# Token loads in 1 KB pieces and whole-array spare matmuls in the head of a fused attention + SwiGLU kernel

## The chip, the cores and the metric

The kernel runs on one core of one Trainium2 chip. A core has five engines that run side by side, each with its own in-order instruction stream: TensorE (PE in the profile, with its weight loads as PEld), VectorE (DVE), ScalarE (ACT), GpSimd (POOL) and SyncE (SP), which here only issues DMAs. The metric is the device time of one execution in microseconds (us); lower is better. The time of the kernel before is 1207.22 us, the median of three runs (1205.26 to 1208.33).

## The reference

One input x of 2048 tokens by 512 features (bf16) goes through a layer norm, and its result xn through two blocks whose outputs are added to x:

```python
xn = _layernorm(x, axis=-1)
return x + _A_ref(xn, A_wqkv, A_wo) + _B_ref(xn, B_w1, B_w3, B_w2)
```

Block A is attention with 32 heads of 16 features: `qkv = xn @ wqkv`, softmax of `q k^T / 4` over all 2048 keys for each head, times v, then `@ wo`. Block B is a gated MLP with 1792 hidden features: `(silu(xn @ w1) * (xn @ w3)) @ w2`. No position enters anywhere, so a fixed permutation of the tokens changes nothing but the place of the output rows.

## The kernel before

**Tiling.** The tokens are 16 tiles of 128. Scores are made twice. In the first pass ("p1") a tile of 128 queries stands as weights and the keys stream past; DVE takes the maximum of each row out of PSUM (line 1040, one reduce for 1024 score columns, 1018 reduces in the record). The maxima go as two more rows into the queries, so that in the second pass ("p2", line 1262) the scores come out transposed and shifted, and ACT only has to take the exponential (lines 1275 and, for two PSUM banks at once, 1305). Then TensorE multiplies with V, and FFN and output matmuls fill what time TensorE has left. The work is cut into units, (query chunk of 512, group of 4 heads, query range); the first three units of the kernel are 128, 128 and 256 queries of the first group.

**Who sets the order.** The order of every engine's instructions is computed when the kernel is built, by a list planner inside `_build`. It keeps a clock per engine (`P.free`), a cost for each instruction (`occ`, `lat`, `_c_mm` and its like for matmuls) and a readiness for each datum, and in a loop it takes from the candidates of all engines (`pick_dve`, `pick_act`, `pick_pe`, `pick_pool`, `pick_sp`) the one that can start first. On the chip each engine then runs its list in order, and semaphores keep the data right; an instruction that the planner expected early and that is late holds up all behind it on its engine.

**The head.** SP issues the loads in this order: token tiles 0-1, 2-3, 4-7 (`load_x`, line 472), the weights of K and of Q (line 476), token tiles 8-11, 12-15, the weights of V; then the first two tiles of x for the residual (`load_xr`, line 845), four pieces of FFN weights and four DRAM fills (lines 493 and 496). For each load the planner adds its KB over `DMA_RATE` (GB/s) to a running landing time that begins at `DMA_FIRST`:

```python
def load(fn, keys, kb):
    landed[0] += kb / DMA_RATE
    P.dma(fn, writes=keys, lat=max(2.2, landed[0] - P.free["sp"]), occ=0.54)
```

Layer norm statistics of tiles 0 to 7 are on DVE (`bn_stats`, line 576, `bn_aggr`, line 579), those of tiles 8 to 15 on ACT (two sums, lines 566 and 570); POOL makes the factors (lines 589 and 592), DVE normalises tiles 0 to 7 (line 605) and POOL the others (line 615). TensorE transposes a normalised tile (line 638), ACT copies it to `xnT` (line 645). With tiles 0 to 3 there, TensorE makes K (`KT0`) and Q (`QT0`) of the first group for the first 512 tokens, four column groups of 32 at a time (line 545, `col_groups`), ACT copies them (lines 661 and 757), and the first p1 scores (line 1000) and the first reduce (line 1040) follow.

**Spare matmuls.** While TensorE has nothing to do ahead of `QT0`, the planner gives it matmuls whose results nobody reads (`warm_cand`, called by `fill_cand` and `pick_pe`): on a free bank, the all-ones tile as weights and as data. Each is one planner item of a column group, that is four matmul instructions of 128x32 weights and 128 columns, each with its weight load, which run side by side in the four column strips of the array. The planner counts `_c_mm(128)`, doubled before its time 5.9 (`_COLD`). `note_load` keeps a sliding sum of streamed columns; ahead of `QT0` nothing is decided by it.

**Which token is where.** Tile t holds in partition p the token 512*(t//4) + 4*p + t%4. Two neighbouring tiles of a load are then 2 KB in a row in DRAM for each partition, four are 4 KB. `load_xr` and `store` move one tile each, with 1 KB per partition, 4 KB apart in DRAM.

## Time and profile before

| what | value |
| --- | --- |
| median of three runs | 1207.22 us (1205.26 to 1208.33) |
| the profiled execution | 1208.99 us |
| its span, first to last instruction | 1207.3 us |
| mean granted TensorE clock | 0.996 of full |
| busy: TensorE, DVE, ACT, POOL | 96%, 97%, 97%, 38% of the span |
| DMA packets, bytes | 129842, 52.90 MB |

The profile is one execution on the chip. "Busy" is the time in which an engine has an instruction in work; a busy TensorE need not be at its peak. A row of the costly groups gives line, engine, operation, output and input with their shapes, and a count, then busy time, mean length in ns, and the idle time of that engine just before these instructions with what ended it. "issue" as that releaser means that the engine waited for nothing that the profile shows. The granted clock is what the throttle left of TensorE's full speed.

### The profile page before, as it was taken

To read this page: it belongs to the slowest core of one execution; us is meant where nothing else is said; L and a number is where in the kernel's file an instruction comes from. 1 tells how busy PE (TensorE), PEld (TensorE's weight loads), DVE (VectorE), ACT (ScalarE), POOL (GpSimd) and SP (SyncE) were. 2 spreads that over 40 slices of the span, in tenths; PEclk is the share of its full clock that TensorE was granted. 3 is DMA by queue.
4 is the path that set the end of the run, shared out by engine and by line. 5 is a ranking of instruction groups with operands and counts; after the bars stand their busy time and mean duration, and the time that the engine had idled before them with its cause. 6 is when DMAs were issued, how large, how long until landed. Compare 5 with 4: busy or idle time off the path is not lost.

```text
span 1207.3 us, 45302 instructions
## 1 busy us (share of the span) xinstructions
PE 1153.4 (96%) x19827; PEld 482.5 (40%) x19827; DVE 1174.8 (97%) x1069; ACT 1176.5 (97%) x2307; POOL 455.1 (38%) x908
## 2 busy tenths in 40 slices
PE   7999999999999999999999999999999999999997
PEld 4444343343334443443333333333333333345554
DVE  5999999999999999999999999999999999999994
ACT  5899999999999999999999999999999999999997
POOL 3435554535322245454222146553122126233320
PEclk8999999999999999999999999999999999999999
DMA  5342313222101122121001112211000111000000
GB/s 171 106 73 65 88 37 92 49 54 52 30 20 29 36 50 53 39 54 29 22 16 27 37 43 66 47 41 34 22 21 16 36 38 34 23 22 21 23 12 25
DMA packets 129842, 52.90 MB, mean 44 GB/s; under 512 B 100084, under 2 KB 129004, under 8 KB 129644
## 3 DMA queue, kind: packets, MB, share of 16 engines
q1 hardware_dynamic: 129644, 50.01, 16.5%
q8 instruction: 155, 2.54, 0.9%
q14 instruction: 43, 0.35, 0.1%
HBM read 38.73 MB, written 6.74 MB: 38 GB/s over the span
## 4 chain that ended last, share of the span: by engine, by line
PE 40%; ACT 40%; DVE 15%; issue 3%; POOL 2%; DMA 1%; ACTq 0%; SPq 0%; POOLq 0%
ACT PT L1275 29%; PE ps L545 22%; DVE part L1040 14%; PE ps L1262 11%; PE ps L1000 6%; ACT PT L1305 4%; ACT th L815 1%; ACT zg L817 1%; ACT ub L821 1%; ACT U L1370 1%; ACT kq L716 1%; POOL a L802 1%; DMA PT<-in_A_x_dram 1%; PE ps L638 0%; POOL Rc L1395 0%
## 5 line engine op out<-in xcount | busy, mean ns | idle before, releaser
L1040 DVE TENSOR_REDUCE part<-ps 128x2 f32<-128x1024 f32 x1018 | 1154.8, 1213 | 9.9 <-PE ps L1000 7.4
L1275 ACT ACTIVATE PT<-ps 128x512 bf16<-128x512 f32 x1824 | 955.1, 629 | 3.8 <-PE ps L1262 2.0
L1262 PE MATMUL ps<-QT,KT 32*128 32x256 bf16 (+1 forms) x4672 | 539.8, 259 | 4.2 <-ACT PT L1305 2.0
L1000 PE MATMUL ps<-KT,QT 32*128 32x512 bf16 x2042 | 431.1, 383 | 2.0 <-DVE part L1040 1.8
L1262 PEld LDWEIGHTS ps<-QT,KT 32*128 32x128 bf16 x4672 | 205.0, 92 | 228.1 <-issue 103.3
L545 PE MATMUL ps<-xnT,ident 128*32 128x512 bf16 (+1 forms) x2476 | 186.6, 353 | 18.7 <-ACT PT L1305 9.2
L1395 POOL TENSOR_TENSOR Rc<-Lc,mone 128x8 f32<-128x8 f32 (+1 forms) x70 | 106.0, 1515 | 254.0 <-DMA Lc<-U 254.0
L545 PE MATMUL ps<-PT,Vaug 128*17 128x256 bf16 (+1 forms) x4672 | 180.8, 261 | 6.1 <-ACT PT L1275 1.6
L545 PE MATMUL ps<-xnT,w 128*32 128x256 bf16 (+1 forms) x2416 | 161.8, 329 | 8.3 <-ACT zg L817 5.8
L1000 PEld LDWEIGHTS ps<-KT,QT 32*128 32x128 bf16 x2042 | 110.2, 91 | 118.9 <-issue 54.0
L545 PEld LDWEIGHTS ps<-PT,Vaug 128*17 128x17 bf16 x4672 | 86.7, 89 | 89.2 <-issue 59.1
L1305 ACT ACTIVATE PT<-ps 128x1024 bf16<-128x1024 f32 x112 | 112.2, 1046 | 0.6
L545 PEld LDWEIGHTS ps<-xnT,ident 128*32 128x32 bf16 x2476 | 50.2, 94 | 96.2 <-ACT PT L1275 41.4
L545 PEld LDWEIGHTS ps<-xnT,w 128*32 128x32 bf16 x2416 | 48.3, 94 | 91.7 <-issue 59.3
L802 POOL TENSOR_TENSOR a<-zg,ub 128x512 f32<-128x512 bf16 x56 | 64.7, 1155 | 27.8 <-ACT ub L821 27.6
L545 PE MATMUL ps<-w,hT 128*32 128x512 bf16 (+1 forms) x1136 | 74.4, 339 | 0.0
L1147 POOL TENSOR_TENSOR mx<-part 128x16 f32<-128x16 f32 (+1 forms) x67 | 14.2, 212 | 155.6 <-DVE part L1040 155.4
L804 POOL TENSOR_TENSOR hT<-a,t 128x512 bf16<-128x512 f32 x56 | 71.2, 1271 | 2.7
L1415 POOL TENSOR_TENSOR wk_on<-U,R 128x256 bf16<-128x256 f32 (+1 forms) x37 | 23.4, 633 | 117.3 <-DMA R<-rd 117.3
L1415 POOL TENSOR_TENSOR on_b<-U,R 128x256 bf16<-128x256 f32 (+1 forms) x33 | 23.5, 712 | 93.4 <-DMA R<-rd 93.4
L800 POOL TENSOR_SCALAR t<-th 128x512 f32<-128x512 bf16 x56 | 34.8, 621 | 8.9 <-ACT th L815 7.0
L817 ACT ACTIVATE zg<-ps 128x512 bf16<-128x512 f32 x56 | 36.4, 650 | 0.0
(98 smaller groups left out, 550.7 us busy)
## 6 DMA issues: line engine op xcount, KB each, us to landing
w<-in_B_w_dram SPq DMA_DIRECT2D x112, 128.0 KB
R<-rd SPq DMA_DIRECT2D x55, 128.0 KB
QT<-qd SPq DMA_DIRECT2D x31, 128.0 KB
KT<-kd SPq DMA_DIRECT2D x28, 128.0 KB
xr<-in_A_x_dram SPq DMA_DIRECT2D x16, 128.0 KB
out_dram<-osb SPq DMA_DIRECT2D x16, 128.0 KB
qd<-kq SPq DMA_DIRECT2D x15, 128.0 KB
w<-in_B_w_dram SPq DMA_DIRECT2D x1, 1792.0 KB
```

Of the source, the lines that this page charges most:

```text
L545: ins = e.matmul(bank(bk)[32 * i:32 * i + m, c0 + a:c0 + b], make_lhsT(i), rhs if (a, b) == (0, ncols) else rhs[:, a:b], start=start, stop ...
L800: q.append(_Item(lambda e: e.tensor_scalar(t1[:, :], th[:, ss, :], 1.0, 1.0, ALU.mult, ALU.add), [("th", ss)], [("t1",)], 0.62, 0.72))
L802: q.append(_Item(lambda e: e.tensor_tensor(a32[:, :], zg[:, ss, :], ub[:, ss, :], ALU.mult), [("zg", ss), ("ub", ss)], [("a32",)], 1.1, 1.25))
L804: q.append(_Item(lambda e: e.tensor_tensor(hT[:, hslot(idx), :], a32[:, :], t1[:, :], ALU.mult), [("a32",), ("t1",)], [("hT", hslot(idx))] ...
L817: _Item(lambda e: e.activation(zg[:, ss, :], bank(bk), ACTF.Identity, scale=0.5), [("ps", bk)], [("zg", ss)], _c_act(512), cb=part_done, n ...
L1000: ins = e.matmul(bank(2 * sl + i), QT[32 * j:32 * j + 32, qs, q * 128:(q + 1) * 128], KT[32 * j:32 * j + 32, g, c_ * 512:(c_ + 1) * 512], ...
L1040: redq.append(_Item(lambda e: e.tensor_reduce(dst, pair_ap.rearrange("p (a b) -> p a b", b=512), AX.X, ALU.max), writes, [("part", par, qt ...
L1262: ins = e.matmul(bank(b)[:, i * nq:(i + 1) * nq], KT[32 * j:32 * j + 32, g, (k0 + i) * 128:(k0 + i + 1) * 128], QT[32 * j:32 * j + 32, qs, ...
L1275: expq.append(_Item(lambda e: e.activation(PT[:, sl, :], bank(b), ACTF.Exp, scale=SCALE), [("ps", b)], [("PT", sl)], _c_act(512), cb=cb, e ...
L1305: return _Item(lambda e: e.activation(PT[:, s0:s1 + 1:s1 - s0, :], ps8[:, b0:b1 + 1, :], ACTF.Exp, scale=SCALE), [("ps", b0), ("ps", b1)], ...
L1395: poolq["nrm"].append(_Item(lambda e: e.tensor_tensor(Rc[:, pp, 0:nl], Lc[:, pp, 0:nl], mone[:, 0:nl], ALU.pow), [("Lc", pp), ("mone",)], ...
L1415: poolq["nrm"].append(_Item(lambda e: e.tensor_tensor(onorm[ob][:, g, q0:q0 + nq], U[:, us, 0:nq], R[:, pp, 0:nq], ALU.mult), [("U", us)] ...
```

## The change

Four things change.

1. Tile t now holds in partition p the token 128*t + p. A tile is 128 KB in a row in DRAM, and each partition's piece of it is one row of 1 KB; a load of two or four tiles has two or four such pieces for each partition. `load_x`, `load_xr` and `store` take the new view.
2. The planner's numbers for the loads: `DMA_FIRST` 3.05 to 3.1, `DMA_RATE` 360 to 341, and 128 KB for a tile where it counted 116 (loads of two) or 111 (loads of four).
3. A spare matmul ahead of `QT0` is one instruction: the whole 128x128 array has ones as weights, and 256 columns stream (the 128 columns of ones twice). The planner counts `_c_mm(256)` for it, and 1024 columns where it counted 512. The spare matmuls of later (`fill_cand` past `QT0`) stay as they are.
4. With these numbers the planner computes the order of all engines anew.

```diff
-    DMA_FIRST = 3.05
-    DMA_RATE = 360.0
+    DMA_FIRST = 3.1
+    DMA_RATE = 341.0
...
-        x_v = A_x[0].rearrange("(a p r) d -> p a r d", p=128, r=4)
-        out_v = out[0].rearrange("(a p r) d -> p a r d", p=128, r=4)
+        x_v = A_x[0].rearrange("(t p) d -> p t d", p=128)
+        out_v = out[0].rearrange("(t p) d -> p t d", p=128)
...
         def load_x(t0, t1):
-            r0 = t0 % 4
-            load(lambda e: e.dma_start(x_sb[:, t0:t1, :], x_v[:, t0 // 4, r0:r0 + t1 - t0, :]),
-                 [("PT", t) for t in range(t0, t1)], (116 if t1 - t0 < 4 else 111) * (t1 - t0))
+            load(lambda e: e.dma_start(x_sb[:, t0:t1, :], x_v[:, t0:t1, :]),
+                 [("PT", t) for t in range(t0, t1)], 128 * (t1 - t0))
...
-            later_dma(lambda e: e.dma_start(xr[:, tg % NXR, :], x_v[:, tg // 4, tg % 4, :]), [], [("xr", tg % NXR)],
+            later_dma(lambda e: e.dma_start(xr[:, tg % NXR, :], x_v[:, tg, :]), [], [("xr", tg % NXR)],
...
-            later_dma(lambda e: e.dma_start(out_v[:, tg // 4, tg % 4, :], osb[:, tg % 4, :]), [("osb", tg % 4)], [("out", tg)],
+            later_dma(lambda e: e.dma_start(out_v[:, tg, :], osb[:, tg % 4, :]), [("osb", tg % 4)], [("out", tg)],
...
         def warm_cand():
-            t = P.free["pe"]
...
                 def emit():
-                    P.pe(col_groups(bk, lambda i: ones_t[:, 32 * i:32 * i + 32], lambda i: ones_t[:, :], 128),
-                         [("ones_t",)], writes, "col", None, _c_mm(128), name="fill")
-                    note_load(st, 512)
+                    P.pe(lambda e: e.matmul(bank(bk)[:, 0:256], ones_t[:, :],
+                                            ones_t[:, :].unsqueeze(1).broadcast_to([128, 2, 128]),
+                                            start=True, stop=True),
+                         [("ones_t",)], writes, "col", None, _c_mm(256), name="fill")
+                    note_load(st, 1024)
                     n_fill[0] += 1
-                return st, emit, _c_mm(128)
+                return st, emit, _c_mm(256)
```

## The prediction

> **What bounds the kernel now.** I read the page first, then a table of stretches, then the head in order of time, then the DMA queues inside the head. The page gives the two engines that are full (first row: the span; second: busy time and share of each engine), and in its list of costly groups the row maxima, which VectorE (DVE) takes.

> ```profile
> span 1207.3 us, 45302 instructions
> PE 1153.4 (96%) x19827; PEld 482.5 (40%) x19827; DVE 1174.8 (97%) x1069; ACT 1176.5 (97%) x2307; POOL 455.1 (38%) x908
> L1040 DVE TENSOR_REDUCE part<-ps 128x2 f32<-128x1024 f32 x1018 | 1154.8, 1213 | 9.9 <-PE ps L1000 7.4
> ```

> The reader is to see that 1018 reduces fill DVE for 1154.8 us and that of their 9.9 us of waiting 7.4 lie at one place, the first one. The table of stretches (columns: length, then busy time and count of PE, PEld, DVE, ACT, POOL, then granted clock, DMA share, GB/s) says where both engines have slack:

> ```profile
> 0.00:22.05 22.05, 13.61 (x399) 9.97 (x400) 9.51 (x27) 7.88 (x16) 5.19 (x20) 0.85 0.74 228
> 22.05:60.00 37.95, 37.86 (x614) 16.09 (x613) 37.62 (x35) 31.80 (x73) 18.09 (x32) 1.00 0.28 84
> ```

> ```profile
> 22.05:1175.00 1152.95, 1113.87 (x18619) 456.29 (x18619) 1150.45 (x1023) 1142.92 (x2250) 447.59 (x884) 1.00 0.17 41
> ```

> DVE works 9.51 of the first 22.05 us, and 1150.45 of the 1152.95 us up to 1175: 2.5 us idle. ACT has 10 us idle there. From the first reduce at 22.05 the kernel runs at DVE's pace, and what ends the head earlier ends the kernel earlier by as much. The head in order of time (start, length, instruction, and in brackets the idle time before it with its releaser), first to 12 us, then from there:

> ```profile
> 2.40 4.40 PE L545 MATMUL ps<-ones_t 128*32 128x128 bf16 x208
> ...
> 8.00 0.69 DVE L576 BATCH_NORM_STATS2 stats<-PT 128x6 f32<-128x512 bf16 x1 [1.42 <-DMA PT<-in_A_x_dram]
> ...
> 9.13 0.40 PE L638 MATMUL ps<-ident,osb 128*128 128x128 bf16 x4 [2.33 <-DVE osb L605]
> ...
> 9.96 1.27 PE L545 MATMUL ps<-ones_t 128*32 128x128 bf16 x52
> ```

> ```profile
> 11.60 1.10 ACT L645 ACTIVATE xnT<-ps 128x512 bf16<-128x512 bf16 x2 [0.29 <-PE ps L638]
> ...
> 11.99 1.12 PE L545 MATMUL ps<-ones_t 128*32 128x128 bf16 x65
> ...
> 13.87 0.19 ACT L566 ACTIVATION_READ_ACCUMULATOR a<-PT 128x1 f32 x1
> ...
> 16.79 0.30 PE L545 MATMUL ps<-ones_t 128*32 128x128 bf16 x3 [3.68 <-issue]
> ...
> 16.80 3.70 PE L545 MATMUL ps<-xnT,wk_on 128*32 128x512 bf16 x32
> ...
> 20.54 0.60 ACT L757 ACTIVATE QT<-ps 128x512 bf16<-128x512 f32 x1 [1.02 <-PE ps L545]
> ...
> 21.40 0.61 PE L1000 MATMUL ps<-KT,QT 32*128 32x512 bf16 x4
> ...
> 22.05 8.09 DVE L1040 TENSOR_REDUCE part<-ps 128x2 f32<-128x1024 f32 x7 [7.44 <-PE ps L1000]
> ```

> Two delays stand out. Token tiles 4 to 7 land at 8.00, and the in-order DVE holds the normalisation of tile 0 behind their statistics. And TensorE stops at 13.11 for 3.68 us with "issue" as releaser: it waits for nothing that the profile shows. It stops inside a spare group: 65 matmuls are sixteen groups of four and one more, and the missing 3 open the next row. No semaphore stands inside a group, and the data of KT0 were there: the last copy of xnT ended at 12.70. So **TensorE had no instructions.** The count of matmuls per stretch (PE alone, then clock, DMA share, GB/s), the page's instruction queue, and three looks of 0.2 us at that queue (7.8 to 8.0, 14.0 to 14.2, 18.6 to 18.8; packets, MB, share) fit:

> ```profile
> 2.00:6.90 4.90, 4.51 (x209) 1.00 0.80 269
> 6.90:13.10 6.20, 3.83 (x141) 1.00 1.06 382
> ```

> ```profile
> q8 instruction: 155, 2.54, 0.9%
> ```

> ```profile
> q8 instruction: 1, 0.02, 32.0%
> ...
> q8 instruction: 1, 0.02, 34.0%
> ...
> q8 instruction: 1, 0.02, 27.4%
> ```

> ```profile
> 7.00:8.00 1.00, 0.00 (x0) 0.00 (x0) 0.00 (x1) 0.00 (x0) 0.00 (x0) 1.00 1.10 376
> ...
> 10.00:11.00 1.00, 0.86 (x52) 0.72 (x52) 1.00 (x5) 0.93 (x3) 0.10 (x1) 1.00 1.04 405
> ...
> 15.00:16.00 1.00, 0.00 (x0) 0.00 (x0) 0.00 (x0) 0.00 (x0) 0.00 (x0) 0.72 0.79 173
> 16.00:17.00 1.00, 0.21 (x7) 0.20 (x10) 0.00 (x0) 0.00 (x0) 0.00 (x0) 0.50 0.34 81
> ...
> 22.00:23.00 1.00, 1.00 (x20) 0.76 (x20) 0.95 (x1) 1.00 (x4) 0.00 (x0) 0.87 0.01 4
> ```

> It falls to 0.50 in the hole and returns after 22: KT0, QT0 and the first scores run at half speed.

> **The change part by part.** *Spare matmuls.* Of the 350 matmuls 16 are transposes and one the mask row, so 333 are spare: with the 3 behind the hole 84 groups of four, 672 instructions with their loads. A new one streams 256 columns where a group streamed 128, and counts so in the plan, so about 42 take their place, 45 with a rounding at each gap: 90 instructions. At KT0 TensorE has then used some 125 instead of 700. KT0 and QT0 add 64; the first 256 are used up at about 17 us, and at the pace of 22.05 to 60 (614 matmuls, 1228 instructions in 37.95 us, 32 per us) the next 256 last 8 us. The slowest block to see is the one of the hole: TensorE had used 418 by 6.90, its 512th fell into the row of 52 that begins at 9.96, around 10.9, and it went on at 16.79: 5.9 us. So the stop goes: **-3.68 us.** Bounds: 0, if the block is late whatever was used, to -3.68. I take the whole.

> *Clock.* The chain of waits has the same work at both clocks:

> ```profile
> 16.79 3.71 PE ps L545 x35
> ...
> 21.47 0.55 PE ps L1000 x4
> ...
> 23.90 0.32 PE ps L1000 x2
> 24.22 0.87 PE ps L545 x16
> ```

> Sixteen matmuls are 0.87 us at full clock, the 32 of KT0 and QT0 1.74, against 3.71 now: **-1.97.** The first scores begin at 21.40 and release DVE at 22.05, 0.65 us; at the row of 0.32 and as much for the way to DVE as now that is about 0.45: **-0.2.** Bounds of both: 0, if the clock is still low, to -2.2. The gap that stays ahead of 9.13 (2.33 us, grown below to 2.7) left the clock at 1.00; I take the full gain.

> *Loads in 1 KB pieces.* A DMA piece was 2 KB (two tiles) or 4 KB (four). The queue in the stretches 2 to 4 us (2 KB), 7 to 8 us (nearly all 1 KB, from the weights) and 10 to 11 us (mostly 4 KB):

> ```profile
> DMA packets 232, 0.43 MB, mean 217 GB/s; under 512 B 24, under 2 KB 24, under 8 KB 232
> ...
> DMA packets 335, 0.38 MB, mean 376 GB/s; under 512 B 13, under 2 KB 324, under 8 KB 334
> ...
> DMA packets 136, 0.40 MB, mean 405 GB/s; under 512 B 11, under 2 KB 46, under 8 KB 136
> ```

> With the shares above, 376/1.10 is 342 GB/s for 1 KB and 405/1.04 is 389 for 4 KB. The 1.05 MB of tiles 0 to 7 then take 3.07 instead of 2.70 us: **+0.4** on the landing at 8.00. Lower end 0, if the queue is not the limit. Upper end +2.2: from 2 to 4 us it moved only some 116 packets per us, and if packets and not bytes set that, the 256 more of the first two loads cost 2.2; the 335 in one us speak against it, so I take the value of the nearer row. [...]

> The order in DVE's queue stays. The plan expects tiles 4 to 7 at 3.1 + 8*128/341 = 6.10 instead of 5.57; DVE is free in the plan at about 6.47, so the statistics of tile 4 are again ahead of the normalisation of tile 0, and the 1.13 us from 8.00 to 9.13 only move. KT0 then begins at 9.13 + 0.4 + 3.98 (to 13.11, spare time unchanged), about 13.5. ACT's two sums of tiles 8 and 9 end at 14.06 now, so the copy of KT0 is not held up by them, also 0.4 later. The loads of xr and the stores had 1 KB pieces before, only of other rows. The xr loads are hidden (no engine's list of waits names xr); the last store is bare and ends the span:

> ```profile
> 1205.02 0.33 SPq L868 DMA_DIRECT2D out_dram<-osb  x1
> ```

> From its issue to 1207.3 are 2.3 us; with the 12% between the two rates above as bound it is +-0.3, and I take 0.

> *The order, computed anew.* The plan chooses every instruction after the head afresh. DVE idles 2.5 us from 22.05 to 1175, so a new order can win 2.5 at most; losing is open. The waits on TensorE that a new order may move in front of DVE, and DVE's own:

> ```profile
> PE ps L545 <- ACT PT L1305: 10.5, 36, 0.5
> ...
> PE ps L1262 <- issue: 1.6, 1, 1.6
> ```

> ```profile
> DVE part L1040 <- PE ps L1262: 2.0, 3, 1.5
> ```

> (The columns are us in total, times, longest.) Bounds -2.5 to +10.5; nearest is DVE's own wait of 2.0, half of which I add: **+1.0.**

> **Sum.** -3.68 - 1.97 - 0.2 + 0.4 + 1.0 = -4.45 us. The profiled execution took 1208.99 us for its span of 1207.3, 1.7 around it; by the sum it would take 1204.5. It is 1.8 us above the median of the three runs, 1207.22, so for the median I get 1202.8. If profiling itself made the hole longer, that is at most these 1.8 us.

> **The rivals.** *The hole stays.* It ends when the bulk loads end: the DMA share falls from 0.79 to 0.34 between the stretches 15 to 16 and 16 to 17 us. If those loads hold TensorE's block back however few instructions it has used, -3.68 and -2.2 are lost and +0.4 + 1.0 remain: 1208.6. The change would then not do what it says. Against it: the stop comes at 700 instructions and inside a group, and at 32 per us TensorE never again waits for "issue" over 1.6 us. [...] Chance 0.09.

> *The clock falls earlier.* If the tokens come at the upper end, +2.2, the gap ahead of the first transposes is 2.33 + 2.2 = 4.5 us, longer than the hole that cost the clock. Then the clock's -2.2 is lost, and the spare work from 9.13 to 13.11 runs at half speed: 125 matmuls, 31 groups, at some 0.055 each (16 groups in about 0.9 us of the row of 65) 1.7 us more. -3.68 + 2.2 + 1.7 + 1.0 = +1.2: 1208.4. It decides from a gap of about 3.7 us, tokens 1.4 late. For it: 2.3 us after TensorE stopped at 13.11 the clock was down already (0.72 in the mean of 15 to 16). Against: the gap of 2.33 left it at 1.00. Chance 0.10.

> *The new order costs more than the head gives.* In TensorE's in-order queue a tile's matmul that waits for a paired exp (L1305) stands ahead of the scores that DVE reduces next. These 36 waits sum to 10.5 us and are hidden now, because DVE has a second pair of banks to reduce meanwhile, 1.13 us (1154.8 over 1018). If the new order puts all of them where that pair is used up, +10.5 stands in place of my +1.0: -5.45 + 10.5 = +5.05, 1212.3, slower. It decides from 5.45 us, half of these waits, and shows as slower from 9.1. For it: DVE and ACT have 0.2% and 0.9% of slack, and 1018 reduces meet new neighbours. Against: the longest such wait is 0.5 us, under one reduce. Chance 0.13.

> **How the numbers follow.** The forecast, hole and low clock gone, has 0.68. A measurement of this kernel tells about 0.3%, 3.6 us, from no change; that is 1203.6 below and 1210.8 above. Of the forecast I put 0.53 below 1203.6 (it needs 3.6 of the 4.45, so it fails where the order costs 1.9 or more, or the hole was 0.9 shorter without the profiler) and 0.15 above. With the first two rivals within 0.3% are 0.34; slower is the third, 0.13. The range goes down to loads that cost nothing and an order that gains 1.0 (-5.65 - 0.2 - 1.0 = -6.85: 1200.4) and up over the first two rivals to 1208.8; left out are the third and a little of the low end.

> **What would show it.** The profile of the changed kernel should have some 45 spare matmuls of 128x256 ahead of KT0 and no wait for "issue" over 1 us before the first reduce; a clock of 1.00 from KT0 to the first scores; the statistics of tile 4 released by the DMA at about 8.4; KT0 at about 13.5 and the first reduce at about 16.6; and from there DVE idle for 2 to 4 us up to 1170. I am wrong if the stop comes back at the end of another block, if the gap before 9.5 brings the clock to 0.50, or if the time from the first reduce to the end, 1185.25 us now, grows by more than 2.

## The result and the profile after

The changed kernel takes 1200.59 us (median of 5 runs, 1199.78 to 1203.1) against 1207.73 us of the kernel before (5 runs beside them, 1205.26 to 1208.33): a ratio of 0.994 with a 95% interval of 0.9922 to 0.9959, 7.1 us or 0.6% faster. The forecast was 1202.8 in a range of 1200.4 to 1208.8, faster as the likeliest case. The profiled execution took 1203.1 us, the longest of the five; a second profile of the same kernel is among the experiments, and the two together show more than either.

The page after: the span, the row of busy times, and the group of reduces (line numbers behind 472 are one less than before).

```profile
span 1201.3 us, 44716 instructions
PE 1153.0 (96%) x19534; PEld 481.6 (40%) x19534; DVE 1174.6 (98%) x1069; ACT 1176.2 (98%) x2307; POOL 453.6 (38%) x908
L1039 DVE TENSOR_REDUCE part<-ps 128x2 f32<-128x1024 f32 x1018 | 1154.7, 1213 | 3.8 <-PE ps L999 1.9
```

TensorE has 293 matmuls less and as many weight loads less, 586 instructions. The 1018 reduces take 1154.7 us where they took 1154.8; the idle time ahead of them is 3.8 us where it was 9.9. The head in order of time:

```profile
2.40 4.80 PE L1614 MATMUL ps<-ones_t 128*128 128x256 bf16 x27
8.27 0.69 DVE L575 BATCH_NORM_STATS2 stats<-PT 128x6 f32<-128x512 bf16 x1 [1.95 <-DMA PT<-in_A_x_dram]
9.40 1.03 PE L637 MATMUL ps<-ident,osb 128*128 128x128 bf16 x8 [2.21 <-DVE osb L604]
10.23 1.70 PE L1614 MATMUL ps<-ones_t 128*128 128x256 bf16 x7
12.57 1.21 PE L1614 MATMUL ps<-ones_t 128*128 128x256 bf16 x9
13.71 1.91 PE L544 MATMUL ps<-xnT,wk_on 128*32 128x512 bf16 x32
16.33 0.40 PE L999 MATMUL ps<-KT,QT 32*128 32x512 bf16 x4 [0.15 <-ACT QT L756]
16.75 10.35 DVE L1039 TENSOR_REDUCE part<-ps 128x2 f32<-128x1024 f32 x9 [1.88 <-PE ps L999]
```

No bracket names "issue" any more: the stop of 3.68 us is gone. KT0 and QT0 (32 matmuls) take 1.91 us where they took 3.70. The first reduce starts at 16.75, 5.30 us earlier than at 22.05; the span ends 6.0 earlier. But the row at 9.40 hides something: eight transposes take 1.03 us, and seven spare matmuls 1.70. By the microsecond (TensorE's busy time and count, clock, DMA share, GB/s) it shows:

```profile
7.00:8.00 1.00, 0.19 (x2) 1.00 1.03 311
...
9.00:10.00 1.00, 0.60 (x6) 0.64 1.10 375
10.00:11.00 1.00, 1.00 (x9) 0.50 1.07 359
...
12.00:13.00 1.00, 1.00 (x12) 0.65 1.10 346
13.00:14.00 1.00, 1.00 (x16) 1.00 1.12 334
```

In this execution the clock was at 0.50 from about 9.4 to 12.6, behind 2.2 us without a matmul, and back at 1.00 as KT0 began. So even this is not the best that the head can do.

**A second stop in the kernel before.** The comparison of the two traces shows one more thing, far behind the head: in the kernel before, TensorE and then DVE stood still between 66 and 69 us (timeline of before, the rows with idle time; then TensorE by stretches of 2 us, columns as above):

```profile
67.97 0.32 PE L1262 MATMUL ps<-QT,KT 32*128 32x128 bf16 x3 [1.61 <-issue]
...
69.20 6.97 DVE L1040 TENSOR_REDUCE part<-ps 128x2 f32<-128x1024 f32 x6 [1.45 <-PE ps L1262]
```

```profile
62.00:64.00 2.00, 2.00 (x36) 1.00 1.14 122
64.00:66.00 2.00, 2.00 (x42) 1.00 0.87 73
66.00:68.00 2.00, 0.39 (x7) 1.00 0.36 68
```

This is the same thing in small: no semaphore is waited for, and a bulk load (w2, 1792 KB, DMA share over 1) has just gone by. In the trace after there is no such row.

**The order.** The planner computed its order anew, and it came out the same: aside from the spare matmuls of the head, every instruction of every engine stands in its place. So what changed behind the head is not due to order, only to when instructions, data and clock are there.

### The profile page after: what moved, and what is told of

Same layout as the page of the kernel before. It is cut to its first block, busy times and chain, and to the rows that moved or that the text cites. A ratio compares the mean times of both kernels' runs of the same rounds, so it can differ in the third digit from the quotient of the medians.

```text
span 1201.3 us, 44716 instructions
## 1 busy us (share of the span) xinstructions
PE 1153.0 (96%) x19534; PEld 481.6 (40%) x19534; DVE 1174.6 (98%) x1069; ACT 1176.2 (98%) x2307; POOL 453.6 (38%) x908
## 3 DMA queue, kind: packets, MB, share of 16 engines
q1 hardware_dynamic: 131052, 50.01, 16.6%
## 4 chain that ended last, share of the span: by engine, by line
ACT 44%; PE 41%; DVE 11%; issue 2%; DMA 1%; POOL 1%; SPq 0%; ACTq 0%; POOLq 0%
ACT PT L1274 32%; PE ps L544 23%; PE ps L1261 11%; DVE part L1039 11%; PE ps L999 6%; ACT PT L1304 5%; ACT th L814 2%; ACT zg L816 2%; ACT ub L820 1%; ACT kq L715 1%; ACT U L1369 1%; DMA PT<-in_A_x_dram 1%; PE ps L637 0%; DMA Lc<-U 0%; POOL a L801 0%
## 5 line engine op out<-in xcount | busy, mean ns | idle before, releaser
L1039 DVE TENSOR_REDUCE part<-ps 128x2 f32<-128x1024 f32 x1018 | 1154.7, 1213 | 3.8 <-PE ps L999 1.9
L544 PE MATMUL ps<-xnT,ident 128*32 128x512 bf16 (+1 forms) x2476 | 186.9, 353 | 18.6 <-ACT PT L1304 9.2
```

The lines of the kernel that those rows point to most:

```text
L544: ins = e.matmul(bank(bk)[32 * i:32 * i + m, c0 + a:c0 + b], make_lhsT(i), rhs if (a, b) == (0, ncols) else rhs[:, a:b], start=start, stop ...
L1039: redq.append(_Item(lambda e: e.tensor_reduce(dst, pair_ap.rearrange("p (a b) -> p a b", b=512), AX.X, ALU.max), writes, [("part", par, qt ...
```

## The experiments

The theory: TensorE's instructions come in blocks of 256 over the DMA engines (in the kernel before the queue q8 moved 155 packets of 16 KB, 64 bytes for each of TensorE's 39654 matmuls and weight loads); a block that is needed while a bulk load fills these engines comes late and TensorE stops (at the first stop the packet moved from 14.10 to 15.19 us, at a DMA share of 1.02, and TensorE went on at 16.79). An edge is the place in the stream where one block ends and the next begins. Fewer instructions ahead of KT0 take away the first stop; that the edges fall elsewhere behind the head takes away the second. The main rivals: the loads in 1 KB pieces make the gain; or it is the shape of the spare matmuls; or the bulk loads stop TensorE whatever it has used. All kernels were timed in 5 rounds beside the kernel before, whose median in the three sets was 1207.68, 1207.79 and 1207.87.

| kernel | median us (range) | ratio to before, 95% | stops for "issue" | first reduce |
| --- | --- | --- | --- | --- |
| spare matmuls alone | 1202.26 (1200.21 to 1205.09) | 0.9959 [0.9945, 0.9973] | none | 15.58 |
| loads alone | 1206.37 (1204.87 to 1212.17) | 0.9992 [0.9977, 1.0007] | 1.18 + 1.98 | 22.07 |
| strips of 256 columns | 1200.63 (1199.33 to 1203.18) | 0.9946 [0.9934, 0.9959] | none | 16.30 |
| bulk loads later | 1205.23 (1203.06 to 1207.87) | 0.9981 [0.9971, 0.9990] | 0.18 + 0.59; 1.06 at 63 | 18.15 |
| weights first | 1202.79 (1201.64 to 1203.16) | 0.9953 [0.9941, 0.9966] | 0.26 at 61 | 13.33 |
| edges moved | 1205.41 (1204.33 to 1208.95) | 0.9985 [0.9975, 0.9995] | 1.96 + 1.36 | 20.00 |
| edges back | 1200.74 (1199.48 to 1202.81) | 0.9939 [0.9927, 0.9952] | 1.22 at 60 | 15.26 |
| the changed kernel again | 1199.89 (1199.75 to 1200.48) | 0.993 [0.9915, 0.9945] | none | 14.50 |
| gap filled | 1200.97 (1200.48 to 1206.43) | 0.9952 [0.9935, 0.997] | 1.38 at 62 | 15.42 |
| w2 later | 1205.19 (1201.6 to 1206.68) | 0.9973 [0.996, 0.9986] | none | 14.94 |

**1. Spare matmuls alone.** The kernel before, with only the new spare matmuls (part 3 of the change):

```diff
-                    P.pe(col_groups(bk, lambda i: ones_t[:, 32 * i:32 * i + 32], lambda i: ones_t[:, :], 128),
+                    P.pe(lambda e: e.matmul(bank(bk)[:, 0:256], ones_t[:, :],
+                                            ones_t[:, :].unsqueeze(1).broadcast_to([128, 2, 128]),
+                                            start=True, stop=True),
```

> The kernel before with only the spare matmuls changed (41 single ones of 256 columns instead of 336 strip matmuls); loads, their numbers and the rest of the order are those of before. Supply theory (TensorE had run out of instruction blocks): no wait for issue over 1 us before the first reduce, KT0 at about 13.3, first reduce at about 16.4, time 0.4 us under the changed kernel, about 1200.2 us (before 1207.7). Rival, the loads did it: the stop of 3 to 4 us stays and the time is 1206.5 to 1208.

It took 1202.26 us, -5.4. The stop is gone with the old loads (timeline):

```profile
12.53 1.91 PE L545 MATMUL ps<-xnT,wk_on 128*32 128x512 bf16 x32 [0.21 <-ACT xnT L645]
...
15.58 9.15 DVE L1040 TENSOR_REDUCE part<-ps 128x2 f32<-128x1024 f32 x8 [0.82 <-PE ps L1000]
```

KT0 waits for data, the last copy of xnT, for 0.21 us, as it should. The second stop is gone as well, with no change to anything near it. I expected about 1200.2, and it is 2 us more. In the profiled execution the clock fell at 1179 to 1187 us, so from the first reduce to the end are 1186.0 us (1201.6 - 15.58), and the span is longer than the head promises. The other runs go the same way: the one with a granted clock of 0.999 took 1200.21 us, the one with 0.994 took 1205.09.

**2. Loads alone.** The changed kernel with the old spare strips, 352 spare matmuls up to KT0:

```diff
-                    P.pe(lambda e: e.matmul(bank(bk)[:, 0:256], ones_t[:, :],
-                                            ones_t[:, :].unsqueeze(1).broadcast_to([128, 2, 128]),
-                                            start=True, stop=True),
+                    P.pe(col_groups(bk, lambda i: ones_t[:, 32 * i:32 * i + 32], lambda i: ones_t[:, :], 128),
```

> The changed kernel with the strip matmuls of before as spare ones (348 of them, four groups more than before because the tokens are expected later). Supply theory: the stop stays, it comes after some 700 instructions, near 13 us, and lasts 3 to 5 us, the clock falls to 0.50; first reduce at 22 to 23.5; time 1207 to 1209 us. Rival, the loads did it: no stop, about 1200.6 us.

It took 1206.37 us; the interval of its ratio includes 1. The stop stays, in two pieces:

```profile
10.88 0.27 PE L637 MATMUL ps<-ident,osb 128*128 128x128 bf16 x2 [1.18 <-issue]
...
17.62 0.46 PE L544 MATMUL ps<-ones_t 128*32 128x128 bf16 x19 [1.98 <-issue]
...
22.07 2.36 DVE L1039 TENSOR_REDUCE part<-ps 128x2 f32<-128x1024 f32 x2 [7.18 <-PE ps L999]
```

The first reduce starts where it did before. So the loads alone do not shorten the head; what is left of 1.3 us is answered by experiment 5.

**3. Strips of 256 columns.** The kernel before, with the spare work still in four strips, but of 256 columns: half the instructions, the same shape.

```diff
-                    P.pe(col_groups(bk, lambda i: ones_t[:, 32 * i:32 * i + 32], lambda i: ones_t[:, :], 128),
+                    P.pe(col_groups(bk, lambda i: ones_t[:, 32 * i:32 * i + 32],
+                                    lambda i: ones_t[:, :].unsqueeze(1).broadcast_to([128, 2, 128]), 256),
```

> The kernel before with the spare matmuls still in four column strips, but 256 columns long: 164 of them, 328 instructions with their loads instead of 672, about 390 used at KT0. Supply theory, by count: the third block is asked for at about 10.5 us and needed after 512 instructions, at about 17 to 18 us, so at most a short stop there (0 to 1 us), and the time is 1200 to 1201.5 us. Rival, the shape (strips against whole array) decides: the stop of about 3.7 us at 13 us stays and the time is about 1207.5 us.

It took 1200.63 us with 164 spare matmuls in place of 333 and no stop, in the head or behind it. It is the number of instructions that decides, not the shape of the array that they use.

**4. Bulk loads later.** The kernel before, with the ten loads for the residual, the FFN weights and the DRAM fills held until KT0 is copied:

```diff
+        def hold():
+            return kh_keys(0, 0)
...
-                      [], [("w13", sl, 0)])
+                      hold(), [("w13", sl, 0)])
```

> The kernel before, same order on every engine, but the residual tokens, the first FFN weights and the four DRAM fills (10 DMAs, 1.3 MB) wait on SyncE until ACT has copied KT0; the spare strip matmuls stay. Supply theory with the block held back by bulk DMAs in the queues: the block asked for at about 10.9 us comes as soon as the weights of V are in, near 13 us; the stop shrinks from 3.7 to between 0.3 and 1.5 us, the clock stays at 1.00, first reduce 17 to 18.5, time 1201.5 to 1204. Rival, a block always takes its 6 us from the request: the stop stays 3.7 us and the time 1207 to 1208.5.

It took 1205.23 us, a smaller gain than expected. The stop shrinks with the queue (0.18 and this one), though TensorE has used as many instructions as before:

```profile
15.06 0.23 PE L550 MATMUL ps<-ones_t 128*32 128x128 bf16 x3 [0.59 <-issue]
...
18.15 6.88 DVE L1045 TENSOR_REDUCE part<-ps 128x2 f32<-128x1024 f32 x6 [3.58 <-PE ps L1005]
```

So the stop needs both, the count and the queue. I expected 1201.5 to 1204. The gain is smaller because the second stop stays (1.06 us at 63.38, DVE 0.90); that the clock was at 0.50 from 11 to 13 us in the profiled execution, behind a pause of 1.54 us, may have added to it.

**5. Edges moved.** The kernel before, with four more groups of strips (32 instructions) in the first spare stretch:

```diff
+                    f = col_groups(bk, lambda i: ones_t[:, 32 * i:32 * i + 32], lambda i: ones_t[:, :], 128)
+                    reps = 5 if n_fill[0] == 10 else 1
```

> The kernel before with 16 more spare matmuls (32 more instructions of TensorE) in the first spare stretch and everything else in the same order: the edges of TensorE's instruction blocks of 256 fall 32 instructions earlier in the work behind it. If the second stop of the kernel before (1.61 us at 66.4, right behind the load of w2) is there because an edge falls behind that load, it goes and the first one stays at 3 to 4 us: about 1206.2 us. If the loads of tokens, not the edges, gave the 1.3 us by which the kernel with the loads alone was faster, it stays at 1207.7.

It took 1205.41 us, where I expected about 1206.2: more spare work and 2.4 us less time, which no account of TensorE's work could give. The first stop stays, in two pieces, and behind the head DVE no longer waits (timeline of DVE, the reduces from 50 to 110 us, one row without a bracket):

```profile
10.33 0.23 PE L545 MATMUL ps<-ones_t 128*32 128x128 bf16 x2 [1.96 <-issue]
...
16.69 0.46 PE L545 MATMUL ps<-ones_t 128*32 128x128 bf16 x19 [1.36 <-issue]
```

```profile
50.72 60.18 DVE L1040 TENSOR_REDUCE part<-ps 128x2 f32<-128x1024 f32 x53
```

From the first reduce to the end of the span are 1183.3 us (1203.3 - 20.00), against 1185.25 before: the second stop, 1.45 on DVE, and a little more. It also explains experiment 2, which has as many matmuls and whose 1183.2 (1205.3 - 22.07) is the same. The time alone does not show this, since the head of this profile is shorter too, by 2.05 us (20.00 against 22.05): the clock fell at 11 us, earlier than before, and was back at 1.00 when KT0 began.

**6. Edges back.** The reverse: the changed kernel with 37 short matmuls (32 columns, 74 instructions) that bring the edges to where they fall before.

```diff
+                    short = 37 if n_fill[0] == 26 else 0
+                        for _ in range(short):
+                            e.matmul(bank(bk)[:, 0:32], ones_t[:, :], ones_t[:, 0:32], start=True, stop=True)
```

> The changed kernel with 37 short whole-array matmuls (32 columns, 74 instructions) ahead of the 27th spare matmul, so that the edges of TensorE's instruction blocks fall behind the head where they fall in the kernel before. If the edges decide, a stop of 1 to 1.6 us returns near 61 to 63 us, behind w2's load, and the time is 1201.8 to 1202.3 us. If they do not, no such stop is there and the time stays at 1200.6.

The stop came back, ahead of the same three matmuls of the program as in the kernel before:

```profile
60.64 0.32 PE L1261 MATMUL ps<-QT,KT 32*128 32x128 bf16 x3 [1.22 <-issue]
...
61.88 13.76 DVE L1039 TENSOR_REDUCE part<-ps 128x2 f32<-128x1024 f32 x12 [1.06 <-PE ps L1261]
```

The place and the size are as the theory has them; the time, 1200.74, is not: I expected 1201.8 to 1202.3. The changed kernel took 1200.59 and 1199.89 in its two sets, so the stop shows as 0.15 to 0.85 us and not as 1.2 to 1.7. From the first reduce to the end are 1184.3 us (1199.6 - 15.26), 0.8 more than in experiment 8. The short matmuls also fill the gap of 2.21 us behind which the clock fell to 0.50 in the profile after (0.19 us of it are left, and the clock stayed at 1.00), which may have paid for a part; that part is not settled.

**7. Weights first.** An attempt to go further: the loads in the order tokens 0 to 3, weights of K and Q, then the other tokens, and the planner told the landings seen in the trace after.

```diff
-    LOADS = ("k", "q", 8, 12)
+    LOADS = ("k", "q", 4, 8, 12)
-    DMA_FIRST = 3.1
-    DMA_RATE = 341.0
+    LANDS = (3.65, 4.9, 8.1, 9.7, 11.2, 13.2, 14.5, 16.0)
```

> The changed kernel, with the weights of K and Q loaded ahead of tokens 4 to 15, the planner told the landings measured in the changed kernel's trace, and the order recomputed. If the head's length is worth its full amount (a reduce of scores that starts t earlier ends the kernel t earlier), the first K projection starts near 9.5 us instead of 13.7, the first reduce at 12.5 to 13.5 instead of 16.75, and the time is about 1197 us (1195.5 to 1199.5). If the recomputed order, or the tokens that land later, give it back (tiles 6 to 15 late to their reduces, VectorE idle between 15 and 30 us), the first reduce is early all the same and the time is 1200.6 or more.

The rival held: the first reduce starts at 13.33, and the kernel takes 1202.79 us, more than the changed kernel. DVE after the first reduce:

```profile
13.33 1.23 DVE L1036 TENSOR_REDUCE part<-ps 128x2 f32<-128x1024 f32 x1 [0.57 <-PE ps L996]
14.47 0.73 DVE L601 TENSOR_SCALAR osb<-PT,mv,lnr 128x512 bf16<-128x512 bf16 x2
...
17.45 0.72 DVE L601 TENSOR_SCALAR osb<-PT,mv,lnr 128x512 bf16<-128x512 bf16 x2
...
19.51 4.86 DVE L1036 TENSOR_REDUCE part<-ps 128x2 f32<-128x1024 f32 x4 [0.20 <-PE ps L996]
25.16 18.49 DVE L1036 TENSOR_REDUCE part<-ps 128x2 f32<-128x1024 f32 x16 [0.79 <-PE ps L996]
43.91 2.36 DVE L1036 TENSOR_REDUCE part<-ps 128x2 f32<-128x1024 f32 x2 [0.27 <-PE ps L996]
```

Normalisations of four tiles (1.45 us) that had been done while DVE had nothing else to do now stand between the reduces, and there are 1.26 us of waits (0.20, 0.79, 0.27), which I put down to the tokens that land later without a run that shows it. That is 2.7 us given back for 1.2 us of earlier start (14.50 in experiment 8). Here the engine that sets the pace gained nothing from an early start, because its other work only moved behind it.

**8. The changed kernel again,** without an edit, for a second profile.

> The changed kernel, unchanged, for a second profile. Its profiled execution of 1203.1 us was the longest of its five and had TensorE at half clock from 9.4 to 12.7 us, behind 2.2 us without a matmul. If that fall is something that happens in some executions only, this profile may have the clock at 1.00 through the head: the first K projection then starts near 12.1 instead of 13.7, the first reduce near 15.1 instead of 16.75, and the span is 1198 to 1199. If the fall belongs to the kernel, the head is as it was and the other executions gained elsewhere.

Six runs from 1199.75 to 1200.48. The head without the fall of the clock (timeline, then TensorE by stretches):

```profile
8.12 0.72 PE L637 MATMUL ps<-ident,osb 128*128 128x128 bf16 x8 [0.68 <-DVE osb L604]
...
11.41 1.91 PE L544 MATMUL ps<-xnT,wk_on 128*32 128x512 bf16 x32
...
14.50 2.35 DVE L1039 TENSOR_REDUCE part<-ps 128x2 f32<-128x1024 f32 x2 [0.90 <-PE ps L999]
```

```profile
7.00:9.00 2.00, 1.32 (x15) 1.00 1.08 366
9.00:11.00 2.00, 2.00 (x22) 1.00 1.10 354
11.00:13.00 2.00, 1.87 (x35) 1.00 1.10 348
```

The tokens landed 1.28 us earlier than in the profile after (statistics of tile 4 at 6.99 against 8.27), so the gap was 0.68 us and the clock stayed. From the first reduce to the end are 1183.5 us (1198.0 - 14.50), as in experiment 3 (1183.5) and near experiment 5 (1183.3).

**9. Gap filled.** The changed kernel with 7 more spare matmuls (14 instructions) in the gap.

```diff
+                    more = 7 if n_fill[0] == 26 else 0
```

> The changed kernel with 7 more spare matmuls ahead of the 27th, so that TensorE is busy until about 8.6 us, when the first tile is ready to be transposed. If the gap of 2.2 us is what lowers the clock, it never falls in the head, no execution is as long as 1203 us, and the median is 1199.5 to 1200.5. If the clock falls for another reason, executions of 1202 to 1203 us stay among them.

This went wrong: 1200.97 us, and runs up to 1206.43, worse than without them. In its profile the head kept its clock, but a stop came at an edge behind w2's load, at another place of the program than before, and the clock fell to 0.50 behind it:

```profile
62.81 0.40 PE L544 MATMUL ps<-hT,xnT 128*32 128x512 bf16 x3 [1.38 <-issue]
```

```profile
62.00:64.00 2.00, 1.19 (x21) 1.00 0.17 53
64.00:66.00 2.00, 1.88 (x58) 0.64 0.24 68
66.00:68.00 2.00, 2.00 (x42) 0.50 0.21 66
```

From the first reduce to the end are 1187.1 us (1202.5 - 15.42), 3.6 more than in experiment 8. Four of the seven runs took 1200.48 to 1200.97, which suggests that the stop does not come in each. Whether the gap causes the long runs of the changed kernel this does not settle, since it changed two things at once; it shows what a block that comes late can cost.

**10. w2 later.** Experiment 6 with the load of w2 issued behind the copies of the second K projection; all engines but SP keep their order.

```diff
-            later_dma(lambda e: e.dma_start(w2[:, :, :], w2_v), [], [("w2",)], lat=12.0)
+            later_dma(lambda e: e.dma_start(w2[:, :, :], w2_v), [], [("w2",)], lat=12.0,
+                      pred=lambda: P.free["sp"] > 62)
```

> The changed kernel with the 37 short matmuls of the run before, in which a stop of 1.22 us came back at 60.6 us, and with w2's load of 1.8 MB issued behind the copies of the second K projection, some 15 to 20 us later; every other instruction in its place. If the block is late because w2's load is ahead of it, there is no stop at 59 to 61 us (a stop may come later, behind the moved load), and the time is 1199.5 to 1200.3 if none comes. If the edge alone makes the stop, it stays at 1.2 us at 60.6, and the time at 1200.7.

With the same edges and w2's load out of the way the stop is gone: DVE reduces from 45.64 to 81.98 without a wait. So the load is needed for it, as in the head. The time is worse all the same, 1205.19 us where I expected 1199.5 to 1200.3, for another reason: the moved load of 1792 KB now stands ahead of the small transfers of the softmax sums (2 and 64 KB).

```profile
78.73 0.45 POOL L1415 TENSOR_TENSOR on_b<-U,R 128x128 bf16<-128x128 f32 x1 [5.42 <-DMA R<-rd]
```

```profile
45.64 36.34 DVE L1040 TENSOR_REDUCE part<-ps 128x2 f32<-128x1024 f32 x32
83.95 2.52 DVE L1040 TENSOR_REDUCE part<-ps 128x2 f32<-128x1024 f32 x2 [1.97 <-PE ps L1000]
```

POOL waits 5.42 us for them (0.78 in experiment 6), its gate products are late, ACT and TensorE stop, and the clock falls to 0.50 between 84 and 90 us.

**What the stops have in common.** The traces hold a stricter test of the theory than the times. These are TensorE's matmuls from the start of the span to just before the end of a stop (busy time and count, clock, DMA share, GB/s): two stops of the kernel before, two of experiment 2, then experiments 6 and 9.

```profile
0.00:16.70 16.70, 8.36 (x350) 0.96 0.85 266
0.00:67.90 67.90, 57.83 (x1112) 0.95 0.50 136
```

```profile
0.00:10.80 10.80, 5.00 (x223) 1.00 0.77 240
0.00:17.60 17.60, 9.76 (x350) 0.90 0.87 257
```

```profile
0.00:60.60 60.60, 56.60 (x856) 1.00 0.57 152
```

```profile
0.00:62.75 62.75, 57.84 (x856) 1.00 0.58 147
```

All twelve stops of these traces (two in the kernel before, the others in the table above) come after 223, 350, 856 or 1112 matmuls (855 in experiment 7), whatever the kernel and the place in its program. Counted with the weight loads and the few waiting instructions of TensorE's queue, that is 449, 705, 1729 and 2241 records, which are whole multiples of 256 apart. So the stops stand at the edges of blocks. The DMA records show what decides at an edge: in these twelve the block's packet ended at most 1.41 us before TensorE reached the edge, or behind it, and TensorE went on 1.2 to 1.7 us after that end. For the edge behind w2's load, in us from the first reduce:

| trace | edge before it passed | packet ended | edge reached | stop |
| --- | --- | --- | --- | --- |
| before | 36.63 | 44.71 | 43.93 | 1.61 |
| edges back (6) | 36.49 | 43.93 | 43.79 | 1.22 |
| edges moved (5) | 35.74 | 40.04 | 42.81 | none |
| loads alone (2) | 35.90 | 39.93 | 42.97 | none |
| changed kernel, two profiles | 38.68, 38.67 | 43.96, 44.04 | 46.03, 46.02 | none |
| gap filled (9) | 38.19 | 45.95 | 45.63 | 1.38 |

The changed kernel too has an edge there, and its block is in time by 2.0 us, some 0.6 us more than the largest lead at which a stop still came. In experiment 9 TensorE is at the edge 0.4 us earlier, but the packet ends 1.9 us later than in experiment 8: so the 14 instructions alone do not explain that stop, and why w2's load held the block longer stays open.

None of these beats the changed kernel.

## Why the prediction was right

**The hole, -3.68.** Right, with its reason, and the counts of matmuls at the stops leave little room for another. The stop went when the instructions went (experiments 1 and 3), stayed when the loads alone changed (2), and shrank when the queue was cleared instead (4). The estimate of 45 spare matmuls was 43. The rival that the bulk loads stop TensorE whatever it has used falls with experiment 1. An edge by itself need not stop TensorE: in the second profile of the changed kernel the list of TensorE's waits up to 1150 us has none for "issue". Behind a bulk load TensorE stopped for 3.68 and 1.61 us (before), 1.22 (experiment 6) and 1.38 (experiment 9).

**The clock, -2.2.** Right in size: KT0 with QT0 takes 1.91 instead of 3.70 us (-1.79), and in the second profile KT0 to first reduce takes 3.09 us (14.50 - 11.41) where it was 5.26: -2.17. But the step that the gap of 2.3 to 2.7 us leaves the clock at 1.00 failed in the profile after, where the clock fell behind a gap of 2.21, one of the prediction's own signs of being wrong. In the kernel before it did not fall behind 2.33, nor in experiment 1 behind 2.45. So a gap of this length can cost the clock and need not. What decides between the two no run here shows.

**The loads, +0.4.** Not seen. The statistics of tile 4 start at 8.00, 8.14, 7.52, 7.96 and 7.39 in five profiles with the old loads (before and experiments 1, 3, 4, 5), and at 8.27, 8.28, 7.70, 6.99, 6.90 and 6.48 in six with the new (after and 2, 6, 8, 9, 10): means of 7.80 and 7.44, each spread over more than the 0.4. That the profile after has 8.27, close to the 8.4 foretold, is therefore luck. I took the rate of 1 KB pieces against 4 KB, but the first loads have 2 KB, and there is no bound by packets either: from 2 to 4 us the queue of the kernel after moves 560 packets where it moved 232.

```profile
DMA packets 560, 0.54 MB, mean 270 GB/s; under 512 B 32, under 2 KB 560, under 8 KB 560
```

These rows show no lower rate for the smaller pieces: 270 GB/s in pieces of 1 KB where it was 217 in pieces of 2 KB.

**The order, +1.0.** Wrong, and the step that failed is the first one: I assumed a new order, and the order came out the same. In its place stands a term that I had in my rows and did not read: the wait for "issue" of 1.6 us and DVE's wait of 1.5 for line 1262 are the second stop, and it is the same mechanism as the first. I used that row only as a bound for a rival. The 586 instructions less move every later edge, the block behind w2's load is in time by 2.0 us, and the stop is not there: -1.45 on DVE, confirmed from both sides (experiments 5 and 6). With it the term is between -1.8 (1183.5 against 1185.25 from the first reduce to the end, second profile) and -0.7 (1184.55, profile after, where the clock fell once more at 197 us).

**The spare time.** One more term was put at nothing: "spare time unchanged", 3.98 us from the first transposes to KT0 without the hole (9.13 to 13.11). It is 3.26, 3.31, 3.34 and 3.29 us in experiments 1, 3, 6 and 8, where the clock stayed: -0.7. In the profile after it is 4.31 (9.40 to 13.71) because of the clock. That KT0 began there at 13.71, near the 13.5 foretold, is two errors that cancel.

**The sum.** Forecast -4.45, measured -7.1 (medians), and -8.0 in the second set (1199.89 against 1207.87). With -3.68 - 2.17 - 0.7 - 1.75 it is -8.3; the loads' share is not resolved. The median lies 0.2 us above the low end of the range, and the second set's lies below it: the first two terms were right, the last two too high by 3.2 us or so, and that the range held is in part luck. The two profiles of the changed kernel, 1203.1 and 1199.85 us, differ by 2.25 us in the head (16.75 against 14.50: the clock and the tokens' landing) and by 1.05 behind it (the clock at 197 us). What stays open: why spare matmuls alone take 1202.26 and with the loads 1199.89 to 1200.59. The rows of the loads show no gain. The runs of experiment 1 are longer where the granted clock is lower, and why it fell in more of them (six runs against eleven) no run here shows; it may be chance.

## What to carry to other kernels

Count a filler's instructions as well as its time: when an engine stands still with "issue" as releaser and a bulk load is in the queue, look for the instruction queue in the list of DMA queues and divide its bytes by the instructions (here 64 for each, 256 in a packet of 16 KB). Count the instructions up to each stop: counts that are whole blocks apart (here 449, 705, 1729 and 2241) say that instructions were late. Fewer, longer instructions ahead of the critical point took the stop of 3.68 us away here (experiments 1 and 3); any change in their number moves every later block edge (32 more took a stop away in experiment 5, 74 more brought one back in experiment 6), so look behind each bulk load for a stop that comes or goes before crediting or blaming the edit itself. Starting the engine that sets the pace earlier is worth its full amount only if the work that filled its waiting time is not pushed behind the start: in experiment 7 it started 1.2 us earlier and 2.7 us were given back.

## What the runs showed of the hardware that was not expected

- A block edge far behind the head cost 1.22 to 1.61 us of TensorE where the packet, behind a 1.8 MB load, ended 0.1 to 0.8 us after the edge was reached (before, experiments 6 and 9), and nothing where the packet ended 2.0 to 3.0 us ahead of it (the changed kernel, experiments 2 and 5): 32 instructions more took such a stop away (experiment 5), 74 more brought it back (experiment 6).
- Pauses of 1.96 (experiment 5) and 2.21 us (after), and one of 1.38 us beside smaller ones (experiment 9), were followed by about 3, 3 and 6 us at a clock of 0.50; other pauses of 2.33 and 2.45 us were not.
- The landing of the same tokens from the same loads varies by at least 1.8 us between profiled executions (the statistics of tile 4 start at 6.48 without a wait in experiment 10, and at 8.28 on their landing in experiment 2), which is as much as the effects that one would like to read from a single profile of the head.
